# Weight conversion through a PSUM bank, its clamp on GpSimd, a small constant summed along a row, and early value products that take turns in one tile

## The chip, the cores and the metric

The kernel runs on one core of a Trainium2 chip. Five engines work there side by side, each through its own list of instructions in the order in which they stand: TensorE (PE in the profile, its weight loads PEld), VectorE (DVE), ScalarE (ACT), GpSimd (POOL) and SyncE (SP, which issues the DMAs). They wait for each other on semaphores. The metric is the device time of one execution in microseconds (us); less is better. Three runs of the kernel before gave 859.16, 859.77 and 861.7 us; the median, 859.77, is the time that the change is held against.

## What is computed

The reference is a local and global attention, whose result goes through a layer of three matrix products under a maximum, and one more product:

```python
s_g = scale * np.matmul(q_g, k_all.transpose(0, 1, 3, 2))        # 32 global queries, all 544 keys
out_g = np.matmul(sm(s_g), v_all)
s_ll = np.where(mask, scale * np.matmul(q_l, k_l^T), -1e9)       # 512 local queries, window of 32
a_l = sm(np.concatenate([s_lg, s_ll], axis=-1))                  # and the 32 global keys
out_l = np.matmul(a_l, np.concatenate([v_g, v_l], axis=2))
x = concat(out_g, out_l) as (8 * 544, 512)
h = np.maximum(np.maximum(x @ w1, x @ w2), x @ w3)               # 512 -> 768
out = h @ w_out                                                  # 768 -> 512
```

There are 8 batches of 8 heads of width 64. `sm` is the softmax, with 1e-9 added to the sum of each row before the division.

## The kernel before

**Places.** The attention is cut into 128 places (`sl` in the loop of line 533): two heads, 128 queries. A place takes the product of queries and keys (`scores`, L339 or L343), mask, minimum and exponent (L346 on DVE, L348 on ACT, which also sums the row into `z`), 1e-9 added to the sum (L350) and its reciprocal (L351), the scaling by it (`times`: L114 on DVE, L116 on ACT or L118 on POOL), a transposition on PE (`trans`, L367) that is copied out of PSUM into `pt`, and the product with the values (`pv`, L405 up to place 25, L412 after it), called PV below. The PV's result lies in the PSUM tile `O`, of two banks, and is copied to `xr` (L105 on ACT or L103 on DVE). `O` has one buffer: the next place's PV waits for that copy. Up to place 25 a PV writes only the first of the two banks. The global queries (`glob`, `glob_soft`, `transg`) go between.

**The layer.** `moe_group` runs the three products (L451), their maximum (L459) and the last product (L470). A matrix is held as a high part that PE's fp32r form takes and a rest (`wh` and `wl`, `woh` and `wol`), so that three matmuls make one product. Its matmuls are dealt out between those of the attention by `fill`; batch 0 goes in two halves of 256 columns, the first from place 8 on.

**The weights.** The 24 pieces (18 for `w1` to `w3`, 6 for `w_out`) come in the first 120 us as raw 64-bit words, two words of 32 bits for each of 512 numbers in 128 rows (`convert`, lines 146 to 168). ACT takes the absolute value of the high words into `wct` (L154). DVE clamps it between 2^-15 and the greatest allowed number (L157), masks and shifts it (L158), joins the sign (L159, written back over the high words of the raw tile `wraw`) and the bits of the low word (L160, into `wct`). ACT rounds the result to fp32r (L163), and POOL subtracts to get the rest (L166). Each call of `weight_step` moves each piece under way by one such step and starts the DMA of another. Three buffers of `wraw` and three of `wct` hold the pieces under way.

**What sets the order.** The code gives the order of the calls. A scheduler then orders each engine's instructions by its own times, with the calls as priorities, and sets the semaphores; it orders accesses of two engines to one tile after one another. Where an engine has a choice (`copy`, `sub`, `times`), the sums kept in `load` by `spend` and `least` choose it when the code is written out.

Of the kernel before, what the change touches and what calls it, by code (L numbers as in the profile page):

```python
# [10 lines left out]
F32 = mybir.dt.float32  # L11
F32R = mybir.dt.float32r
I32 = mybir.dt.int32
BF16 = mybir.dt.bfloat16
AF = mybir.ActivationFunctionType
ALU = mybir.AluOpType
AX = mybir.AxisListType
# [12 lines left out]
HIMAX = float(np.array(0x47EFFFFF, np.int32).view(np.float32))  # L30
# [20 lines left out]
def f32(ap):  # L51
    return ap.bitcast(F32)


def body(ctx, tc, kin, qin, vin, min_, win, out):
    nc = tc.nc
    act, dve, pool, pe = nc.scalar, nc.vector, nc.gpsimd, nc.tensor

    const = ctx.enter_context(tc.tile_pool(name="const", bufs=1))
    att = ctx.enter_context(tc.tile_pool(name="att", bufs=2))  # L60
    xp = ctx.enter_context(tc.tile_pool(name="xp", bufs=4))
    moe = ctx.enter_context(tc.tile_pool(name="moe", bufs=1))
# [3 lines left out]
    psO = ctx.enter_context(tc.tile_pool(name="psO", bufs=1, space=PSUM))  # L66

    small = ctx.enter_context(tc.tile_pool(name="small", bufs=4))
# [10 lines left out]
    def spend(e, ns):  # L79
        load[e] += ns  # L80
# [26 lines left out]
    def times(out, a, col, move=False):  # L107
        n = width(out)
        c = {"d": n * 0.52 + 125, "a": n * 0.833 + 185}
        if not move:  # L110
            c["p"] = n * 1.27 + 150
        e = least(c)
        if e == "d":
            dve.tensor_scalar(out=out, in0=a, scalar1=col, scalar2=None, op0=ALU.mult)  # L114
        elif e == "a":
            act.activation(out=out, in_=a, func=AF.Copy, scale=col)  # L116
        else:
            pool.tensor_scalar(out=out, in0=a, scalar1=col, scalar2=1.0, op0=ALU.mult, op1=ALU.mult)  # L118
# [5 lines left out]
    mask = const.tile([128, 2, 256], BF16, name="mask")  # L124
    zero = small.tile([128, 1], F32, name="zero", bufs=1)
    dve.memset(zero, 0.0)
    s4 = const.tile([128, 4, 2, 256], F32, name="s4")
    pool.memset(s4, 0.0)
    qgz = const.tile([128, 2, 160], F32R, name="qgz")
# [4 lines left out]
    wo = [const.tile([128, 6, DM], F32R, name=t) for t in ("woh", "wol")]  # L134
    xg = const.tile([128, NP, B, SG], F32, name="xg")


    def pieces():
        for n in range(24):
            f, i = divmod(n, 3)  # L140
            if n < 18:
                yield n, *[w[f][:, i].rearrange("p k f -> p (k f)") for w in (wh, wl)]
            else:
                yield n, *[w[:, n - 18] for w in wo]

    def convert(piece):
        m, dh, dl = piece
        r = moe.tile([128, 512], mybir.dt.int64, name="wraw", tag=f"h{3 + m % 3}")
        nc.sync.dma_start(out=r, in_=win[m])
        hi = r.bitcast(I32).rearrange("p (n t) -> p n t", t=2)[:, :, 1]  # L150
        lo = r.bitcast(I32).rearrange("p (n t) -> p n t", t=2)[:, :, 0]
        yield
        c = att.tile([128, 512], I32, name="wct", tag="vs") if m % 3 < 2 else moe.tile([128, 512], I32, name="wct")
        act.activation(out=f32(c), in_=r.bitcast(F32).rearrange("p (n t) -> p n t", t=2)[:, :, 1], func=AF.Abs)  # L154
        spend("a", 620)
        yield
        dve.tensor_scalar(out=f32(c), in0=f32(c), scalar1=2.0 ** -15, scalar2=HIMAX, op0=ALU.max, op1=ALU.min)  # L157
        dve.tensor_scalar(out=c, in0=c, scalar1=0x07FFFFFF, scalar2=3, op0=ALU.bitwise_and, op1=ALU.logical_shift_left)  # L158
        dve.scalar_tensor_tensor(out=hi, in0=hi, scalar=-0x40000000, in1=c, op0=ALU.bitwise_and, op1=ALU.bitwise_or)  # L159
        dve.scalar_tensor_tensor(out=c, in0=lo, scalar=29, in1=hi, op0=ALU.logical_shift_right, op1=ALU.bitwise_or)  # L160
        spend("d", 2300)
        yield
        act.copy(out=dh, in_=f32(c))  # L163
        spend("a", 615)
        yield
        pool.tensor_tensor(out=dl, in0=f32(c), in1=f32(dh), op=ALU.subtract)  # L166
        spend("p", 1350)
        yield True

    todo = pieces()  # L170
# [3 lines left out]
    def weight_load():  # L174
        piece = next(todo, None)
        if piece is not None:
            c = convert(piece)
            next(c)
            loaded.append(c)
# [11 lines left out]

    NAT = 26
    EARLY = 16
    kraw, kst, qraw, qs, vraw, vs, xr, sc, pg, pts, pgt = [{} for _ in range(11)]
    prob = []
    kn, qg = [], []
# [12 lines left out]
    def nat_k(p):  # L209
        if p < NP:  # L210
            return kn[p // 2][:, p % 2], qg[0][:, p]
        return kraw[p][:, 0:KW], kraw[p][:, KW:]
# [23 lines left out]
    def load_q(s):  # L236
        if s >= NS:
            return
        if s < EARLY:
            if s % 2 == 0:  # L240
# [76 lines left out]
    def scores(i):  # L317
        if i >= NS:
            return
        sl = ORDER[i]  # L320
        p, t = divmod(sl, 4)
        c0, n = WIN[t]

        ps = pm.tile([128, 512], F32, name="pm") if i < 8 else psS.tile([128, 512], F32, name="S")
        s = s4[:, i % 4]
        if i < EARLY:
            sc[i] = s
        else:
            if len(prob) < 2:
                prob.append(const.tile([128, 2, 256], F32R, name="prob", tag=f"prob{2 + len(prob)}"))  # L330
                pool.memset(f32(prob[-1]), 0.0)
            sc[i] = prob[i % 2]
        nm = small.tile([128, 2], F32, name="nm")
        z = small.tile([128, 2], F32, name="z")
        ph = [ps[:, 0:224], ps[:, 224:448]]
        for j in range(2):
            if i in NATK:

                pe.matmul(ph[j][:, 0:n], lhsT=qraw[i][:, 128 * j:128 * j + 128], rhs=nat_k(p)[0][:, c0:c0 + n],  # L339
                          start=True, stop=True)  # L340
                continue
            for a in range(2):
                pe.matmul(ph[j][:, 0:n], lhsT=qs[i][:, a, 128 * j:128 * j + 128],  # L343
                          rhs=kst[p][:, j, c0:c0 + n], start=(a == 0), stop=(a == 1))
        for j in range(2):
            dve.tensor_tensor_reduce(out=s[:, j, 0:n], in0=ph[j][:, 0:n], in1=mask[:, (1, 0, 1, 0)[t], 32 * (t == 0):32 * (t == 0) + n],  # L346
                                     scale=-0.125, scalar=3.0e38, op0=ALU.add, op1=ALU.min, accum_out=nm[:, j:j + 1])
            act.activation(out=s[:, j, 0:n], in_=s[:, j, 0:n], func=AF.Exp, bias=nm[:, j:j + 1], scale=-1.0,  # L348
                           accum_out=z[:, j:j + 1])
        dve.tensor_scalar(out=z, in0=z, scalar1=1e-9, scalar2=None, op0=ALU.add)  # L350
        dve.reciprocal(out=z, in_=z)  # L351
        for j in range(2):
            times(s[:, j, 0:n], s[:, j, 0:n], z[:, j:j + 1])
        if i >= EARLY:
            nc.sync.dma_start(out=f32(sc[i])[:, :, 0:n], in_=s[:, :, 0:n])
        spend("d", 2 * (n * 1.04 + 220) + 440)
        spend("a", 2 * (n * 0.833 + 278))

    def trans(sl):
# [3 lines left out]
        ps = psT.tile([128, 512], F32, name="T")  # L363
        pr, one = (ps, ident) if sl < EARLY else (ps.bitcast(F32R), identr)
        for j in range(2):
# [29 lines left out]
    def pv(sl):  # L395
        p, t = divmod(ORDER[sl], 4)
        pt = pts.pop(sl)
        o = psO.tile([128, 2, 512], F32, name="O")
        if t == 0:
            xr[p] = xp.tile([128, 4, 160], F32, name="xr")  # L400
        if sl < NAT:

            for c, j in ((0, 0), (0, 1), (1, 0), (1, 1)):
                n = 160 if c < GCH[t][2] else 128
                pe.matmul(o[64 * j:64 * j + 64, 0, 0:n], lhsT=vraw[sl][:, 2 * j + c], rhs=pt[:, j, c, 0:n], start=(c == 0), stop=(c == 1))  # L405
            copy(xr[p][:, t], o[:, 0, 0:160], True)
        else:

            for j in range(2):
                for c in range(2):  # L410
                    n = 160 if c < GCH[t][2] else 128
                    pe.matmul(o[:, j, 0:320].rearrange("p (a q) -> p a q", a=2)[:, :, 0:n],  # L412
                              lhsT=vs[sl][:, 2 * j + c].rearrange("p a d -> p (a d)"),
                              rhs=pt[:, j, c, :, 0:n], start=(c == 0), stop=(c == 1))
            lo = att.tile([64, 2, 160], F32, name="lox", bufs=1)
            copy(lo, o[64:128, :, 0:160], True)
            spend("d", 460 + 2 * 320)
            dve.tensor_tensor(out=lo, in0=o[0:64, :, 160:320], in1=lo, op=ALU.add)
            for j in range(2):
                dve.tensor_tensor(out=xr[p][64 * j:64 * j + 64, t], in0=o[0:64, j, 0:160], in1=lo[:, j], op=ALU.add)  # L420
        if t == 3:
            dve.tensor_reduce(out=xg[:, p % NP, p // NP], in_=xr[p][:, :, 128:160].rearrange("p t g -> p g t"),
                              axis=AX.X, op=ALU.add)
# [109 lines left out]
    for sl in range(NS):  # L533
        p, t = divmod(ORDER[sl], 4)
# [112 lines left out]
```

## Time and profile before

| what | before |
|---|---|
| median of three runs | 859.77 us |
| the profiled execution | 859.45 us |
| its span, first to last instruction | 857.4 us |
| PE busy | 814.9 us, 95% of the span |
| PE busy in the first 140 us | 106.4 us |
| DVE, ACT, POOL busy | 573.7, 530.8, 517.2 us |
| granted PE clock, mean | 0.981 |

How to read it: the profile is that of one execution. The span is what its instructions cover; 859.45 - 857.4 = 2.05 us lie around it. Busy shares are averages over a start (attention alone, with the weights being converted), a long middle part and an end (the layer alone). An engine's idle time matters only where the engine that sets the end waits for it. "Waited for" and releasers are inferred from the semaphores.

### The profile page before, as it was taken

What the parts mean: (1) busy time and instruction counts of PE and PEld (TensorE: products, weight loads), DVE (VectorE), ACT (ScalarE), POOL (GpSimd) and SP (SyncE); (2) the same over time, 40 slices, a digit from 0 to 9 for tenths busy, and PEclk for the clock granted to TensorE, in tenths of its full rate; (3) what the DMA queues carried; (4) which work ended last, traced back from release to release, by engine and by line L of the source; (5) the groups of instructions that cost most, each with busy time, mean ns of one, the idle gap of its engine ahead of it and who ended that gap; (6) DMA issues with size and microseconds to landing.
All of it is one profiled execution on the core that took longest, in us unless ns stands there. A gap on an engine that the chain in (4) does not pass through costs nothing.

```text
span 857.4 us, 15953 instructions
## 1 busy us (share of the span) xinstructions
PE 814.9 (95%) x4668; PEld 688.3 (80%) x4668; DVE 573.7 (67%) x1806; ACT 530.8 (62%) x1497; POOL 517.2 (60%) x705
## 2 busy tenths in 40 slices
PE   6668779989999999999999999999999999999997
PEld 4447668977888888888888888888888888888896
DVE  5889964587778677777777777867787776511111
ACT  6576555676677766767677767777776776511111
POOL 4578664687667666776678667766677664411211
PEclk9689899999999999999999999999999999999999
DMA  7555434444233533343333423253334332100000
GB/s 267 160 168 189 148 117 139 130 121 136 91 105 97 164 109 112 106 132 118 99 106 121 145 86 100 90 170 103 112 111 137 113 90 69 49 24 1 26 25 25
DMA packets 93414, 94.56 MB, mean 110 GB/s; under 512 B 18448, under 2 KB 81808, under 8 KB 93328
## 3 DMA queue, kind: packets, MB, share of 16 engines
q1 hardware_dynamic: 93328, 93.56, 35.3%
q8 instruction: 37, 0.61, 0.3%
q14 instruction: 49, 0.40, 0.2%
HBM read 56.85 MB, written 8.91 MB: 77 GB/s over the span
## 4 chain that ended last, share of the span: by engine, by line
PE 86%; DVE 7%; DMA 2%; issue 2%; ACT 1%; POOL 1%; SPq 0%; POOLq 0%; DVEq 0%; ACTq 0%
PE pm L451 48%; PE pm L470 16%; PE O L412 6%; PE S L343 5%; PE T L367 4%; PE S L287 2%; PE O L405 1%; DVE wct L160 1%; DVE wraw L159 1%; PE S L339 1%; DVE wct L157 1%; PE S L385 1%; PE S L283 1%; DVE z L350 1%; DVE s L346 1%
## 5 line engine op out<-in xcount | busy, mean ns | idle before, releaser
L451 PE MATMUL pm<-xs,wh 128*128 128x512 f32 (+1 forms) x1440 | 424.6, 370 | 8.8 <-DVE m L459 5.5
L451 PEld LDWEIGHTS pm<-xs,wh 128*128 128x128 f32 x1440 | 255.5, 191 | 40.4 <-DVE m L459 6.2
L451 PE MATMUL pm<-xs,wl 128*128 128x512 f32 (+1 forms) x720 | 266.6, 370 | 4.3 <-POOL wl L166 4.3
L118 POOL TENSOR_SCALAR s<-s,z 128x224 f32<-128x224 f32 (+1 forms) x248 | 114.7, 475 | 82.7 <-ACT lox L105 36.0
L451 PEld LDWEIGHTS pm<-xs,wl 128*128 128x128 f32 x720 | 137.4, 191 | 26.1 <-POOL wl L166 4.7
L470 PE MATMUL pm<-woh,h 128*128 128x512 f32 x408 | 133.7, 399 | 1.6 <-POOL h L97 1.2
L97 POOL TENSOR_TENSOR h<-m,h 128x512 fp32r<-128x512 f32 (+1 forms) x60 | 70.7, 1178 | 98.6 <-ACT h L105 98.5
L348 ACT ACTIVATE s<-s,nm 128x224 f32<-128x224 f32 (+1 forms) x256 | 118.2, 462 | 17.5 <-DVE nm L346 13.5
L459 DVE TENSOR_TENSOR m<-pm,m 128x512 f32<-128x512 f32 (+1 forms) x120 | 72.9, 608 | 71.2 <-PE pm L451 71.0
L97 POOL TENSOR_TENSOR qs<-qraw,qs 128x256 fp32r<-128x256 f32 x100 | 72.8, 738 | 54.7 <-ACT qs L105 45.5
L97 DVE TENSOR_TENSOR pt<-T,pt 128x512 fp32r<-128x512 f32 x102 | 70.4, 690 | 48.0 <-ACT pt L105 45.7
L346 DVE CUSTOM_DVE_ANT_0 s<-S,mask 128x224 f32<-128x224 f32 (+1 forms) x240 | 80.6, 370 | 23.3 <-PE S L339 17.7
L350 DVE TENSOR_SCALAR z<-z 128x2 f32<-128x2 f32 x128 | 55.8, 436 | 52.7 <-ACT s L348 52.5
L470 PEld LDWEIGHTS pm<-woh,h 128*128 128x128 f32 x408 | 74.6, 188 | 13.9 <-POOL h L97 1.7
L470 PE MATMUL pm<-wol,h 128*128 128x512 f32 x204 | 81.9, 401 | 0.0
L97 POOL TENSOR_TENSOR vs<-vraw,vs 128x256 fp32r<-128x256 f32 x102 | 75.5, 740 | 7.1 <-ACT vs L105 3.0
L97 POOL TENSOR_TENSOR kst<-kraw,kst 64x576 fp32r<-64x576 f32 x50 | 71.6, 1431 | 11.0 <-issue 7.0
L105 ACT CAST pt<-T 128x512 fp32r<-128x512 f32 x89 | 52.0, 584 | 39.3 <-PE T L367 39.3
L105 ACT CAST qs<-qraw 128x256 fp32r<-128x256 f32 x100 | 40.7, 407 | 56.1 <-PE S L343 51.8
L412 PEld LDWEIGHTS O<-pt,vs 128*128 128x128 f32 x408 | 66.1, 188 | 8.8
L412 PE MATMUL O<-pt,vs 128*128 128x320 f32 (+1 forms) x408 | 72.8, 300 | 0.0
L343 PEld LDWEIGHTS S<-kst,qs 128*128 128x128 f32 x400 | 59.3, 190 | 9.4 <-DVE nmg L291 1.1
(96 smaller groups left out, 1284.1 us busy)
## 6 DMA issues: line engine op xcount, KB each, us to landing
vraw<-v_in SPq DMA_DIRECT2D x64, 256.0 KB, 3.1
qraw<-q_in SPq DMA_DIRECT2D x100, 128.0 KB, 2.2
prob<-s SPq DMA_DIRECT2D x56, 224.0 KB, 2.4
wraw<-w_in SPq DMA_DIRECT2D x24, 512.0 KB, 3.6
prob<-s SPq DMA_DIRECT2D x56, 192.0 KB, 2.3
out_dram<-o SPq DMA_DIRECT2D x32, 256.0 KB, 2.4
kraw<-k_in SPq DMA_DIRECT2D x25, 320.0 KB, 3.0
qn<-q_in SPq DMA_DIRECT2D x8, 256.0 KB, 5.2
```

The lines of the kernel that those rows point to most:

```text
L97: (dve if least(c) == "d" else pool).tensor_tensor(out=out, in0=a, in1=b, op=ALU.subtract)
L105: act.copy(out=out, in_=a)
L118: pool.tensor_scalar(out=out, in0=a, scalar1=col, scalar2=1.0, op0=ALU.mult, op1=ALU.mult)
L343: pe.matmul(ph[j][:, 0:n], lhsT=qs[i][:, a, 128 * j:128 * j + 128], rhs=kst[p][:, j, c0:c0 + n], start=(a == 0), stop=(a == 1))
L346: dve.tensor_tensor_reduce(out=s[:, j, 0:n], in0=ph[j][:, 0:n], in1=mask[:, (1, 0, 1, 0)[t], 32 * (t == 0):32 * (t == 0) + n], scale=-0.12 ...
L348: act.activation(out=s[:, j, 0:n], in_=s[:, j, 0:n], func=AF.Exp, bias=nm[:, j:j + 1], scale=-1.0, accum_out=z[:, j:j + 1])
L350: dve.tensor_scalar(out=z, in0=z, scalar1=1e-9, scalar2=None, op0=ALU.add)
L367: pe.transpose(pr[:, 256 * j + 128 * c:256 * j + 128 * c + 128], s[:, j, 128 * c:128 * c + 128], one)
L412: pe.matmul(o[:, j, 0:320].rearrange("p (a q) -> p a q", a=2)[:, :, 0:n], lhsT=vs[sl][:, 2 * j + c].rearrange("p a d -> p (a d)"), rhs=pt[ ...
L451: pe.matmul(ps[:, 0:n], lhsT=w[f][:, i, k], rhs=xs[k][:, a, c0:c0 + n], start=(q == 0), stop=(q == 11))
L459: dve.tensor_tensor(out=m[:, 0:n], in0=ps[:, 0:n], in1=m[:, 0:n], op=ALU.max)
L470: pe.matmul(ps, lhsT=hh[f][:, a, 128 * t:128 * t + 128], rhs=w[:, f], start=(q == 0), stop=(q == 17))
```

## The change

Four edits. They are shown whole; the line numbers of the kernel after are larger by 4 to 12.

```diff
+    z8 = small.tile([128, 4, 2, 2], F32, name="z8", bufs=1)
+    dve.memset(z8, 1e-9)
...
+    early_o = psO.tile([128, 2, 512], F32, name="O")
...
-        c = att.tile([128, 512], I32, name="wct", tag="vs") if m % 3 < 2 else moe.tile([128, 512], I32, name="wct")
+        c = att.tile([128, 512], I32, name="wct", tag="vs") if m % 2 else moe.tile([128, 512], I32, name="wct", bufs=2)
...
-        dve.tensor_scalar(out=f32(c), in0=f32(c), scalar1=2.0 ** -15, scalar2=HIMAX, op0=ALU.max, op1=ALU.min)
-        dve.tensor_scalar(out=c, in0=c, scalar1=0x07FFFFFF, scalar2=3, op0=ALU.bitwise_and, op1=ALU.logical_shift_left)
-        dve.scalar_tensor_tensor(out=hi, in0=hi, scalar=-0x40000000, in1=c, op0=ALU.bitwise_and, op1=ALU.bitwise_or)
-        dve.scalar_tensor_tensor(out=c, in0=lo, scalar=29, in1=hi, op0=ALU.logical_shift_right, op1=ALU.bitwise_or)
-        spend("d", 2300)
+        pool.tensor_scalar(out=f32(c), in0=f32(c), scalar1=HIMAX, scalar2=2.0 ** -15, op0=ALU.min, op1=ALU.max)
+        spend("p", 800)
+        yield
+        w = early_o[:, 1].bitcast(I32)
+        dve.tensor_scalar(out=w, in0=c, scalar1=0x07FFFFFF, scalar2=3, op0=ALU.bitwise_and, op1=ALU.logical_shift_left)
+        dve.scalar_tensor_tensor(out=w, in0=hi, scalar=-0x40000000, in1=w, op0=ALU.bitwise_and, op1=ALU.bitwise_or)
+        dve.scalar_tensor_tensor(out=c, in0=lo, scalar=29, in1=w, op0=ALU.logical_shift_right, op1=ALU.bitwise_or)
+        spend("d", 2000)
         yield
...
-        spend("p", 1350)
+        spend("p", 1290)
...
+    EARLY_O = 18
...
+        ze = z8[:, i % 4]
...
-                           accum_out=z[:, j:j + 1])
-        dve.tensor_scalar(out=z, in0=z, scalar1=1e-9, scalar2=None, op0=ALU.add)
+                           accum_out=ze[:, j, 0:1])
+        dve.tensor_reduce(out=z, in_=ze, axis=AX.X, op=ALU.add)
...
-        o = psO.tile([128, 2, 512], F32, name="O")
+        if sl < EARLY_O:
+            o = early_o[:, :, 160 * (sl % 3):160 * (sl % 3) + 160]
+        else:
+            o = psO.tile([128, 2, 512], F32, name="O")
```

The clamp becomes a step of its own on POOL. The three bit operations stay on DVE, but their intermediate result `w` lies in the second bank of a tile `O` that is taken once, for places 0 to 17 together; the PVs of those places write its first bank, at one of three offsets by turns. There are four buffers of `wct` for three. The sum of a softmax row goes into the first of two numbers, the second of which is 1e-9, and a reduction adds the two. The global rows keep their addition (L301).

The scheduler's order is the same on PE from the PV of place 19 on, and changes ahead of that. On VectorE, before, the first conversion stands behind the exponents of the sixth pair of scores, and waits for ScalarE (its absolute value):

```order
L350 TENSOR_SCALAR z<-z 128x2 [waits Activation_49]
L299 TENSOR_TENSOR nmg<-nmg 64x1 [waits DVE_49]
L351 RECIPROCAL z<-z 128x2 [waits DVE_49]
L157 TENSOR_SCALAR wct<-wct 128x512 [waits Activation_49]
L158 TENSOR_SCALAR wct<-wct 128x512 [waits DVE_49]
L346 ISA s_92,nm<-pm,mask 128x192 [waits PE_49,Pool_49]
```

After (L165 to L167 are the three bit operations, L299 is L291 of before, L359 the new reduction; `O` stands for `w` in the second bank):

```order
L299 ISA sg,nmg<-S,zero 64x384 [waits PE_49,Pool_49]
L299 ISA nmg 64x1
L359 TENSOR_REDUCE z<-z_92 128x2 [waits Activation_49]
L299 ISA sg,nmg<-S,zero 64x160 [waits PE_49]
L165 TENSOR_SCALAR O<-wct 128x512 [waits Activation_49]
L360 RECIPROCAL z<-z 128x2 [waits DVE_49]
L166 SCALAR_TENSOR_TENSOR O<-wraw,O 128x512 [waits DMAHW1_49,DVE_49]
L167 SCALAR_TENSOR_TENSOR wct<-wraw,O 128x512 [waits DVE_49]
L165 TENSOR_SCALAR O<-wct 128x512 [waits DVE_49,Pool_49]
```

The first conversion has moved behind the second pair's global scores, and its wait for ScalarE is for the copy of place 2's PV out of the same tile `O`.

On TensorE, in the stretch in which the layer's matmuls have begun, a PV before (L405) waits for ScalarE, which fills `pt`:

```order
L451 MATMUL pm<-xs,wl_103 128x256
L451 MATMUL pm<-xs,wh_97 128x256
L405 MATMUL O<-pt,vraw 64x160 [waits PE_49,Activation_49]
L405 MATMUL O<-pt,vraw 64x160 x3
L451 MATMUL pm<-xs,wh_97 128x256
```

After, the PV (L417) of place 9 stands there, and the layer's matmuls are L463:

```order
L463 MATMUL pm<-xs,wh_100 128x256 x2
L463 MATMUL pm<-xs,wl_106 128x256
L417 MATMUL O<-pt,vraw 64x160 [waits DVE_49]
L417 MATMUL O<-pt,vraw 64x160 x3
L463 MATMUL pm<-xs,wh_100 128x256 x2
L463 MATMUL pm<-xs,wl_106 128x256 [waits Pool_49]
```

The PV now waits for VectorE: for the last bit operation (L167) of the conversion that stands ahead of it, which read the tile's other bank. That holds for the thirteen PVs of places 3 to 15, with 24 conversions between the PV of place 2 and that of place 15.

On VectorE the opposite wait stands after each of these PVs. Around place 8:

```order
L166 SCALAR_TENSOR_TENSOR O<-wraw,O 128x512 [waits DMAHW7_49,DVE_49]
L167 SCALAR_TENSOR_TENSOR wct<-wraw,O 128x512 [waits DVE_49]
L471 TENSOR_TENSOR m<-pm,m 128x256 [waits PE_49,Activation_49]
L471 TENSOR_TENSOR m<-pm,m 128x256 [waits DVE_49,PE_49]
L165 TENSOR_SCALAR O<-wct 128x512 [waits Activation_49,Pool_49]
L166 SCALAR_TENSOR_TENSOR O<-wraw,O 128x512 [waits DMAHW2_49,DVE_49]
```

L165 waits for ScalarE's copy of that PV into `xr`, and for POOL's clamp; between the two conversions stand two maxima of the layer (L471).

## The prediction

> **What bounds the kernel now.** I read the chain that ended last first, by engine, then the engines' busy time by stretch (span, PE, PEld, DVE, ACT, POOL, granted PE clock, DMA share, GB/s).
>
> ```profile
> span 857.4 us, 15953 instructions
> PE 86%; DVE 7%; DMA 2%; issue 2%; ACT 1%; POOL 1%; SPq 0%; POOLq 0%; DVEq 0%; ACTq 0%
> ```
>
> ```profile
> 17.00:122.60 105.60, 78.09 (x494) 61.71 (x492) 92.97 (x221) 67.51 (x185) 74.87 (x82) 0.85 0.49 156
> 27.20:122.60 95.40, 71.14 (x455) 57.34 (x453) 84.45 (x195) 60.88 (x165) 69.19 (x72) 0.86 0.49 156
> 0.00:140.00 140.00, 106.44 (x656) 83.39 (x658) 106.22 (x301) 85.77 (x243) 86.18 (x109) 0.89 0.54 172
> 140.00:200.00 60.00, 55.78 (x424) 49.79 (x421) 40.53 (x154) 41.44 (x130) 43.87 (x65) 1.00 0.42 125
> 200.00:740.00 540.00, 540.00 (x2989) 457.59 (x2988) 406.38 (x1311) 383.77 (x1085) 370.14 (x514) 1.00 0.37 112
> ```
>
> From 200 to 740 us PE is busy without a gap, so whatever the change does to the other engines there costs and gives nothing. PE is idle 33.6 us of the first 140, and in the stretch of the weight conversion (17 to 122.6) DVE is busy 92.97 of 105.6 us. That stretch sets the start; the 7% of DVE in the chain lie there. What DVE does in it by groups (count, busy us, mean ns); then DVE's busy time on the tile `wct` alone, which is the conversion, and last on everything in the first 10.2 us of the stretch:
>
> ```profile
> L160 DVE SCALAR_TENSOR_TENSOR wct<-wraw 128x512 int32<-128x512 int32 x24 | 23.7, 988 | 0.0
> L159 DVE SCALAR_TENSOR_TENSOR wraw<-wraw,wct 128x512 int32<-128x512 int32 x24 | 22.8, 948 | 0.3 <-DVE nm L346 0.2
> L157 DVE TENSOR_SCALAR wct<-wct 128x512 f32<-128x512 f32 x24 | 14.3, 595 | 2.0 <-ACT wct L154 2.0
> L158 DVE TENSOR_SCALAR wct<-wct 128x512 int32<-128x512 int32 x24 | 13.9, 580 | 0.2
> L346 DVE CUSTOM_DVE_ANT_0 s<-S,mask 128x224 f32<-128x224 f32 (+1 forms) x22 | 7.9, 363 | 3.3 <-PE S L339 3.3
> L350 DVE TENSOR_SCALAR z<-z 128x2 f32<-128x2 f32 x14 | 6.9, 491 | 2.2 <-ACT s L348 2.2
> ```
>
> ```profile
> 17.00:27.20 10.20, 5.58 (x7) 0.79 0.50 157
> 17.00:122.60 105.60, 72.44 (x96) 0.85 0.49 156
> ```
>
> ```profile
> 17.00:27.20 10.20, 8.52 (x26) 0.79 0.50 157
> ```
>
> 72.4 of 93 us are conversion. And it is slow for a reason that one place shows (start, duration):
>
> ```profile
> 29.95 0.69 DVE L159 SCALAR_TENSOR_TENSOR wraw<-wraw,wct 128x512 int32<-128x512 int32 x1
> ...
> 35.72 3.85 DVE L159 SCALAR_TENSOR_TENSOR wraw<-wraw,wct 128x512 int32<-128x512 int32 x1
> ```
>
> ```profile
> 35.38 1.17 POOL L118 TENSOR_SCALAR probg<-sg,zg 64x128 f32<-64x128 f32 x3
> 36.52 2.49 POOL L166 TENSOR_TENSOR wl<-wct,wh 128x512 fp32r<-128x512 f32 x2
> ```
>
> The same operation takes 0.69 or 3.85 us; the long one ends at 39.57, one plain duration after POOL's work ended at 39.01. DVE waited for POOL inside the instruction.
>
> **The change part by part.** I follow PE to the PV of place 19, from which PE's order is the same: in before it starts at 139.58. What comes earlier there, comes earlier at the end.
>
> ```profile
> 139.58 0.76 PE L405 MATMUL O<-pt,vraw 128*64 128x160 f32 x8
> ```
>
> Prices of nearest rows (count, busy us, mean ns; the last with min/median/max):
>
> ```profile
> L459 DVE TENSOR_TENSOR m<-pm,m 128x512 f32<-128x512 f32 x84 | 57.9, 689 | 50.0 <-PE pm L451 49.9
> L350 DVE TENSOR_SCALAR z<-z 128x2 f32<-128x2 f32 x128 | 55.8, 436 | 52.7 <-ACT s L348 52.5
> ...
> L346 DVE DVE_READ_ACCUMULATOR2_ANT nm<- 128x1 f32 x256 | 21.0, 82 | 0.0
> L351 DVE RECIPROCAL z<-z 128x2 f32<-128x2 f32 x128 | 21.0, 164 | 3.6
> ...
> L422 DVE TENSOR_REDUCE xg<-xr 128x32 f32<-128x128 f32 x32 | 12.3, 384 | 0.5
> ...
> L103 DVE COPY pt<-T 128x512 f32<-128x512 f32 x1 | 0.7, 692 | 0.6 <-PE T L367 0.6
> ```
>
> ```profile
> L118 POOL TENSOR_SCALAR sg<-sg,zg 64x544 f32<-64x544 f32 x28 | 20.0, 714 | 28.2 <-ACT pt L105 26.0 <-DVE zg L302 1.1 <-ACT sg L300 0.7
> ```
>
> ```profile
> L157 DVE TENSOR_SCALAR wct<-wct x24: 395/416/1860, 17.9 to 114.9; 128x512 f32<-128x512 f32 x24
> L163 ACT CAST wh<-wct x18: 602/619/622, 22.4 to 97.0; 128x512 fp32r<-128x512 f32 x18
> L166 POOL TENSOR_TENSOR wl<-wct,wh x18: 1254/1442/1816, 24.2 to 97.7; 128x512 fp32r<-128x512 f32 x18
> ```
>
> Bit operations. Each now has at most one input in SBUF, as L459 has, whose mean is its plain duration. I take 0.69 for all three (the first between 0.42, the median of such an operation inside SBUF, and 0.69): 24 x 2.07 = 49.7 us for 72.4. The Trainium skill (VectorE: DVE Perf Modes, "Why PSUM operands drop a tier") says that an operand in PSUM costs a 4-byte operation its double rate; by that the low end falls away, and at the low end the sum would be 6.6 us shorter.
>
> Sum of the rows. No row shows a reduction of 2 x 2 numbers; between nothing and 0.38 I take the reciprocal's 0.16, since fixed cost is all that it has: 14 x (0.491 - 0.16) = 4.6 us off DVE. Of the 128 in all, the 114 later ones lie beside a full PE; without that cover they would be worth 30 us ((55.8 - 6.9) - 114 x 0.16).
>
> Other work of DVE from 27.2 on is (92.97 - 72.44) - (8.52 - 5.58) = 17.6 us, less 4.6. By the order four more masked scores stand ahead of the last conversion: 4 x (0.363 + 0.08, the short read that follows each) = 1.8. So DVE has 49.7 + 14.8 = 64.5 us to do. Its idle time of that stretch, 95.40 - 84.45 = 10.95, I keep.
>
> The later start. The first conversion now waits for the copy of place 2's PV, which ended at 27.46 in before:
>
> ```profile
> 27.17 0.29 ACT L105 COPY xr<-O 128x160 f32<-128x160 f32 x1 [3.57 <-PE O L405]
> ```
>
> So I start at 27.5, where before 5.58 us of conversion were done; this is in the sum, since all 24 stand behind it.
>
> The new wait. Conversion and PV exclude each other in the shared tile. A PV waits for L167, with PE's layer matmuls and the next scores queued behind it; the next L165 waits for the copy of that PV, with the maxima and later scores queued on DVE, for which ACT's exponents wait. One such turn in before, PV to copy:
>
> ```profile
> 67.99 0.76 PE L405 MATMUL O<-pt,vraw 128*64 128x160 f32 x8
> ...
> 69.14 0.28 ACT L105 COPY xr<-O 128x160 f32<-128x160 f32 x1
> ```
>
> 1.43 us; with the hand-overs 1.5, thirteen times 19.5. By the order 2 to 8 other instructions of DVE stand between the last conversion ahead of a PV and the next one behind it, and go on meanwhile, so I take half, 9.75 (bounds 0 and 19.5). The offsets by turns save nothing: a PV still waits, now for more.
>
> The clamp on POOL. 24 x 0.71 = 17.0 us (544 columns in 64 rows take 714 ns; no row has a minimum on POOL; at the subtraction's 1.25 it would be 30). POOL had 31 us idle between 17 and 122.6. Behind a clamp queue subtractions and scalings; DVE waits for it. I take a quarter, 4.3, as standing in DVE's way (bounds 0 and 17.0). ACT's added scalings and the memset hide in ACT's and DVE's idle time; a fourth `wct` buffer costs nothing. SP's load of the next `wraw` waits for L167 as it did for L160, with the loads of queries and values behind it: no change.
>
> Sum: 27.5 + 64.5 + 10.95 + 9.75 + 4.3 = 117.0 us for the last subtraction, where before it ended at 122.1:
>
> ```profile
> 120.85 1.28 POOL L166 TENSOR_TENSOR wol<-wct,woh 128x512 fp32r<-128x512 f32 x1
> ```
>
> But PE is then further: by the order 49 matmuls stand between the first that waits for that subtraction and the PV of place 19. In before the PV of place 17 began at 129.69, with 59 matmuls to go, 9.89 us; 49 take 8.2.
>
> ```profile
> 129.69 0.76 PE L405 MATMUL O<-pt,vraw 128*64 128x160 f32 x8
> ```
>
> PE's own 71.1 us at clock 0.86 fit. The PV comes at 125.2 for 139.58, 14.4 us earlier, and PE is full from 200 on: 859.45 - 14.4 = 845.05 for the profiled execution; the median of the runs is 0.32 above it: **845.4 us**.
>
> **The rivals.** Turns uncovered (chance 0.18): all 19.5 us, 9.75 more: 855.2. For it: each engine's order is fixed, so an engine that finds one instruction blocked can't take the next first. Against: the instructions between.
>
> Turns covered (0.15): half of the 14.05 us for turns and clamps goes: 838.4; all of it, 831.4.
>
> The ring, slower (0.11): a piece's clamp stands on POOL behind an earlier piece's subtraction, that behind ACT's rounding, that behind DVE's bit operations, and DVE's next piece waits for the clamp: 0.62 + 1.25 + 0.71 = 2.6 us each turn with nothing between, 33.8 in all in place of the 4.3: 874.9. It decides from 1.6 us of such waiting in each turn on ((14.4 + 2.6 + 4.3)/13). Against: by the order clamps stand a piece or more ahead of their use.
>
> The port pays back (0.06): the 17.0 us given to POOL block DVE for as long, as in the 3.85 us above, instead of 4.3: 858.1, no change. The rows speak against it: few DVE operations of that stretch keep two inputs in SBUF. The Trainium skill (Perfetto Trace Analysis, "Optimizing Scalar/DVE Operations") warns that work moved between GPSIMD and DVE may not help, since they share a read port. The 3.85 us agree with the shared port, not with the conclusion.
>
> **How the numbers follow.** The forecast has 0.50. 0.3%, 2.6 us, is about what a measurement can tell from no change. Faster: 0.50 + 0.18 + 0.15 = 0.83; same 0.06; slower 0.11. The range 836 to 857 leaves out the ring, the port and the far part of covered turns, together 0.2.
>
> **What would show it.** Right: L166 and L167 at 0.69 us with no long ones, the reduction below 0.2, the clamp at 0.7, DVE's conversions near 50 us, the PV of place 19 near 125 and PE full from 200 on. The new wait must show as PE's wait for L167 (DVE) before PVs and DVE's wait for ACT's copy or for POOL before L165. Wrong: bit operations that still stretch to microseconds (the port), DVE waiting for the clamp over 1.6 us a turn (the ring), or a gain in the first 140 us that is lost after it.

## The result and the profile after

The kernel after takes 849.1 us (median of four runs, 849.05 to 850.82), the kernel before on the same chip 859.46 (four runs, 858.21 to 861.7). The ratio is 0.9881, with a 95% interval from 0.9857 to 0.9906: 10.4 us faster. The forecast was 845.4 us, with a range from 836 to 857. The profiled execution of after is its longest run, 850.82 us, 8.6 less than that of before.

The page of after gives its span, and the share by engine of the chain that ended last:

```profile
span 848.8 us, 15999 instructions
PE 81%; DVE 2%; DMA 1%; ACT 1%; POOL 1%; issue 1%; SPq 0%; POOLq 0%; ACTq 0%; DVEq 0%
```

The windows of after (columns as in the prediction: PE, PEld, DVE, ACT, POOL, PE clock, DMA share, GB/s):

```profile
17.00:122.60 105.60, 86.05 (x540) 66.69 (x536) 71.24 (x221) 71.49 (x201) 72.57 (x105) 0.90 0.52 164
27.20:122.60 95.40, 78.27 (x493) 61.29 (x493) 66.15 (x191) 64.11 (x177) 66.41 (x92) 0.91 0.54 170
0.00:140.00 140.00, 115.01 (x724) 88.54 (x726) 85.54 (x297) 90.67 (x260) 88.11 (x137) 0.93 0.56 179
200.00:740.00 540.00, 540.00 (x2985) 457.62 (x2984) 380.50 (x1302) 379.98 (x1077) 365.64 (x509) 1.00 0.36 110
```

DVE lost 21.7 us of work in the conversion stretch (92.97 to 71.24), PE is idle 25.0 us of the first 140 for 33.6, and the long middle is as full as before. The DVE groups of that stretch show why (count, busy us, mean ns; then idle time ahead of them):

```profile
L166 DVE SCALAR_TENSOR_TENSOR O<-wraw,O 128x512 int32<-128x512 int32 x24 | 16.6, 692 | 0.3
L165 DVE TENSOR_SCALAR O<-wct 128x512 int32<-128x512 int32 x24 | 16.6, 690 | 5.9 <-POOL s L118 2.1 <-issue 1.9 <-ACT xr L105 0.9
L167 DVE SCALAR_TENSOR_TENSOR wct<-wraw,O 128x512 int32<-128x512 int32 x24 | 16.4, 683 | 0.4
...
L359 DVE TENSOR_REDUCE z<-z 128x2 f32<-128x4 f32 x17 | 2.6, 151 | 0.2
```

All three bit operations take 0.69 us, each time; nothing is stretched to microseconds. And yet the last subtraction ends no earlier, at 122.64 us for 122.13, and the PV of place 19 comes at 131.02. Its timeline rows on POOL and on PE:

```profile
121.36 1.28 POOL L173 TENSOR_TENSOR wol<-wct,woh 128x512 fp32r<-128x512 f32 x1
```

```profile
131.02 0.76 PE L417 MATMUL O<-pt,vraw 128*64 128x160 f32 x8
```

That PV is 8.56 us earlier than before, and the execution 8.63 us shorter. So the whole gain lies ahead of place 19, as forecast, but it is 8.6 and not 14.4. DVE is now idle for 34 of the 105.6 us, so something besides its work holds up the start.

### The profile page after: what moved, and what is told of

The parts are those of the page before. It is cut to its first block, busy times and chain, and to the rows that moved or that the text cites. A ratio compares the mean times of both kernels' runs of the same rounds, so it can differ in the third digit from the quotient of the medians.

```text
span 848.8 us, 15999 instructions
## 1 busy us (share of the span) xinstructions
PE 814.9 (96%) x4668; PEld 685.8 (81%) x4668; DVE 523.8 (62%) x1784; ACT 530.4 (62%) x1498; POOL 515.4 (61%) x727
## 4 chain that ended last, share of the span: by engine, by line
PE 81%; DVE 2%; DMA 1%; ACT 1%; POOL 1%; issue 1%; SPq 0%; POOLq 0%; ACTq 0%; DVEq 0%
PE pm L463 47%; PE pm L482 15%; PE O L424 6%; PE S L352 5%; PE T L376 4%; PE S L295 2%; DMA prob<-s 1%; PE S L394 1%; PE O L417 1%; PE S L348 1%; ACT s L357 0%; DVE xr L432 0%; DVE pt L97 0%; ACT sg L308 0%; DVE s L355 0%
## 5 line engine op out<-in xcount | busy, mean ns | idle before, releaser
L463 PE MATMUL pm<-xs,wh 128*128 128x512 f32 (+1 forms) x1440 | 419.9, 367 | 2.7 <-ACT wh L170 2.4
L463 PEld LDWEIGHTS pm<-xs,wh 128*128 128x128 f32 x1440 | 252.6, 189 | 33.3 <-ACT wh L170 2.9
L463 PE MATMUL pm<-xs,wl 128*128 128x512 f32 (+1 forms) x720 | 266.0, 370 | 3.9 <-POOL wl L173 3.8
L463 PEld LDWEIGHTS pm<-xs,wl 128*128 128x128 f32 x720 | 136.1, 189 | 25.7 <-POOL wl L173 5.2
L118 POOL TENSOR_SCALAR s<-s,z 128x224 f32<-128x224 f32 (+1 forms) x246 | 105.6, 442 | 63.8 <-ACT lox L105 40.6
L97 POOL TENSOR_TENSOR h<-m,h 128x512 fp32r<-128x512 f32 (+1 forms) x60 | 68.7, 1145 | 99.0 <-ACT h L105 98.7
L471 DVE TENSOR_TENSOR m<-pm,m 128x512 f32<-128x512 f32 (+1 forms) x120 | 73.0, 608 | 77.6 <-PE pm L463 75.5
L432 DVE TENSOR_TENSOR xr<-O,lox 64x160 f32<-64x160 f32 x204 | 64.3, 315 | 3.4
```

What stands on the lines that cost most here:

```text
L97: (dve if least(c) == "d" else pool).tensor_tensor(out=out, in0=a, in1=b, op=ALU.subtract)
L463: pe.matmul(ps[:, 0:n], lhsT=w[f][:, i, k], rhs=xs[k][:, a, c0:c0 + n], start=(q == 0), stop=(q == 11))
L471: dve.tensor_tensor(out=m[:, 0:n], in0=ps[:, 0:n], in1=m[:, 0:n], op=ALU.max)
```

## The experiments

Four theories of what holds it up. A: PE with its own work sets the pace. B: the turns that conversions and PVs take in the shared tile `O`, which nothing covers. C: the clamp delays POOL's subtractions. D: it is still DVE's list of work, as the forecast summed it. Medians with the kernel before on the same chip, and the ratio's 95% interval:

| run | edit | us | before | ratio |
|---|---|---|---|---|
| after | the change | 849.1 | 859.5 | 0.986 to 0.991 |
| e1 | after, bit operations in a bank of their own | 837.1 | 859.6 | 0.972 to 0.975 |
| e2 | after, no clamp | 853.2 | 859.6 | 0.991 to 0.995 |
| e3 | after, two bit operations of three | 838.6 | 859.6 | 0.974 to 0.978 |
| e4 | after, clamp on DVE | 858.9 | 859.6 | 0.998 to 1.001 |
| e5 | e1, two bit operations of three | 838.6 | 860.1 | 0.973 to 0.977 |
| e6 | before, clamp on POOL alone | 862.8 | 860.1 | 1.002 to 1.005 |
| e7 | before, new sum of 1e-9 alone | 856.9 | 860.1 | 0.996 to 0.998 |
| e8 | before, bit operations through a bank of their own alone | 847.7 | 860.1 | 0.983 to 0.988 |
| e9 | e1, clamp on DVE | 846.1 | 859.5 | 0.982 to 0.986 |
| e10 | e1, old sum of 1e-9 | 837.4 | 859.5 | 0.972 to 0.976 |
| e11 | before, the turns alone | 860.3 | 859.5 | 0.999 to 1.002 |

**e1: no turns.**

```diff
...
-    early_o = psO.tile([128, 2, 512], F32, name="O")
+    early_o = psE.tile([128, 512], F32, name="Oe")
+    early_w = psE.tile([128, 512], F32, name="We")
...
-        w = early_o[:, 1].bitcast(I32)
+        w = early_w.bitcast(I32)
...
```

`psE` is a pool of two banks that is closed ahead of place 18, where `psO` opens in its stead.

> The change as it is, but the early value products and the bit operations get a PSUM tile of one bank each, so that neither waits for the other; nothing else is edited. The change as it is: 849.1 us, the value product of place 19 at 131.0 us. Theory A (pace): after the change TensorE with its own work sets the pace from place 7 on (53.8 of 60.5 us busy between the products of places 7 and 15), and the 5.7 us that the forecast lacks lie there; the turns cost only what the trace shows, 1.4 us of TensorE's wait for the last bit operation: 847.5 to 849.5 us, place 19 not before 129. Theory B (turns): the 5.7 us are turns that nothing covers: 843 to 844.5 us, place 19 near 125.

It took 837.1 us, 12 less than the change. Theory A falls at once, as far as the change goes, and the gain is more than twice the 5.7 us that theory B had counted. The windows of e1, up to the end of its last subtraction and over the first 140 us; then that subtraction on POOL and the PV of place 19 on PE:

```profile
27.20:104.90 77.70, 67.64 (x478) 55.46 (x477) 61.37 (x183) 61.81 (x176) 64.61 (x91) 0.96 0.65 201
...
0.00:140.00 140.00, 122.03 (x839) 99.43 (x840) 90.20 (x330) 97.94 (x287) 95.00 (x150) 0.96 0.62 195
```

```profile
103.63 1.28 POOL L176 TENSOR_TENSOR wol<-wct,woh 128x512 fp32r<-128x512 f32 x1 [1.27 <-ACT woh L173]
```

```profile
116.81 0.76 PE L424 MATMUL O<-pt,vraw 128*64 128x160 f32 x8
```

The last subtraction ends at 104.91, 17.7 us earlier than in the change, and place 19 comes 14.2 us earlier, as much as the span is shorter (834.4 for 848.8). DVE's idle time from 27.2 to that subtraction falls from 29.25 (95.40 - 66.15) to 16.33 us (77.70 - 61.37); the other 4.8 us are work of DVE that no longer stands in that stretch. In part that is because e1 starts its first conversion at 19.1 and not at 27.0 us: 2.7 us of conversions lie ahead of 27.2 there, 0.2 in the change. So e1 gives back all that the shared tile costs, the later start with it, and not the turns alone. How the turns cost that much shows in one of them, in the timeline of the change around the PV of place 12 (all engines; the rows between are left out):

```profile
96.06 0.68 DVE L167 SCALAR_TENSOR_TENSOR wct<-wraw,O 128x512 int32<-128x512 int32 x1
...
97.45 0.28 PE L463 MATMUL pm<-xs,wl 128*128 128x256 f32 x1
...
97.66 0.71 PE L417 MATMUL O<-pt,vraw 128*64 128x160 f32 x8
...
98.24 0.67 ACT L158 ACTIVATE wct<-wraw 128x512 f32<-128x512 f32 x1 [0.47 <-DMA wraw<-w_in]
...
98.81 0.28 ACT L105 COPY xr<-O 128x160 f32<-128x160 f32 x1
...
99.18 0.69 DVE L165 TENSOR_SCALAR O<-wct 128x512 int32<-128x512 int32 x1 [0.92 <-ACT xr L105]
```

The conversion lets go of the tile at 96.74, and the next begins at 99.18. In the 2.44 us between, PE first ends the layer's matmuls that stand ahead of the PV, and ACT's copy stands behind an absolute value that waits for its DMA. Little of this is booked as a wait for the turn: PE works, ACT waits for a DMA, and DVE's row shows 0.92 us. So the waits that the profile puts down to the turns are far less than what they cost: 0.9 us of DVE for the copy (the row of L165 above), and of PE and its weight loads for L167 what the view of that line names (who waited, us, times):

```profile
  PEld O L417: 1.8, 2
  PE O L417: 1.4, 2
```

The tile's own account shows it. From the first matmul of place 2's PV to the end of place 15's copy are 97.6 us:

```profile
24.25 0.53 PE L417 MATMUL O<-pt,vraw 128*64 128x160 f32 x1
```

```profile
121.62 0.27 ACT L105 COPY xr<-O 128x160 f32<-128x160 f32 x1
```

Summing from each L165's start to its L167's end, and from each PV's start to its copy's end, the 24 conversions hold the tile for 56.4 us (2.35 each) and the 14 PVs for 21.2 (1.51 each): 77.6 of 97.6 us. That is a larger share than DVE's 66, POOL's 66 or ACT's 64 of 95.4; only PE's 78 is larger, and e1, where place 19 comes 14.2 us earlier, shows that PE could go faster. The rest are hand-overs like this one. In e1 PV and conversion lie side by side:

```profile
73.57 0.71 PE L424 MATMUL Oe<-pt,vraw 128*64 128x160 f32 x8
...
73.72 0.69 DVE L170 SCALAR_TENSOR_TENSOR wct<-wraw,We 128x512 int32<-128x512 int32 x1
...
74.52 0.69 DVE L168 TENSOR_SCALAR We<-wct 128x512 int32<-128x512 int32 x1
...
75.98 0.31 ACT L107 COPY xr<-Oe 128x160 f32<-128x160 f32 x1
```

Here the copy comes 2.41 us after its PV's start, later than in the change, and costs nothing, since DVE goes on. In the change too the two lie in different banks of the tile; it is the scheduler that orders them by the tile. The Trainium skill (PSUM — Partial Sum Buffer, "PSUM bank collisions raise a hardware error") asks for semaphores by bank and quadrant, in the simple version by bank. e1, in which PE and DVE work in two banks at the same time, agrees. The wait gone, the earlier start and the order that the scheduler then writes come together in e1. How much each gives wasn't taken apart.

**e3 and e5: one bit operation less, with and without turns.** Both leave out the second operation, which joins the sign, and book 1310 for 2000 in `spend`.

```diff
...
-        dve.scalar_tensor_tensor(out=w, in0=hi, scalar=-0x40000000, in1=w, op0=ALU.bitwise_and, op1=ALU.bitwise_or)
...
-        spend("d", 2000)
+        spend("d", 1310)
...
```

> The change as it is with one of the three bit operations left out (the second, which joins the sign): VectorE loses 24 x 0.69 = 16.6 us in the conversion. Theory A (pace): VectorE is no longer what bounds the start, so little comes of it: 847 to 849.2. Theory D (the forecast's own sum, VectorE's list as the line that sets the end): 16.6 us less on that line, of which TensorE's idle 6.7 us between places 7 and 15 and what it idles before allow at least 6: 843 or less.

> The kernel of e1 (the change with a PSUM tile of its own for the bit operations, 837.1 us) with the second bit operation left out, as in e3: VectorE loses the same 16.6 us that gave 10.5 us with the shared tile. New theory B (the shared tile is the line that sets the end: it is held 77.7 of the 97.6 us from the value product of place 2 to that of place 15, and e3 gained because each hold became 0.7 us shorter): without the shared tile VectorE's price counts for little: 834 to 837. Theory D (VectorE's list sets the end, with or without turns): about 10 us again: 825 to 829.

With the shared tile it gives 10.5 us (838.6), without it nothing (838.6 for 837.1), about as theory B expected. But this doesn't settle what e3 gained by. The windows of e5 up to the end of its last subtraction and from there to the PV of place 19, those two rows, and the window of e1 between its own two:

```profile
27.20:98.02 70.82, 60.96 (x444) 50.57 (x442) 54.66 (x172) 56.08 (x154) 58.65 (x79) 0.96 0.62 205
98.00:117.80 19.80, 18.07 (x118) 14.57 (x116) 7.07 (x36) 7.72 (x25) 3.16 (x7) 1.00 0.45 135
```

```profile
96.72 1.29 POOL L175 TENSOR_TENSOR wol<-wct,woh 128x512 fp32r<-128x512 f32 x1 [0.49 <-ACT woh L172]
```

```profile
117.80 0.76 PE L423 MATMUL O<-pt,vraw 128*64 128x160 f32 x8
```

```profile
104.90:116.80 11.90, 11.83 (x82) 10.17 (x82) 3.37 (x22) 6.56 (x20) 2.45 (x6) 1.00 0.45 135
```

The last subtraction of e5 ends at 98.01, 6.9 us earlier than in e1; only place 19 comes no earlier (117.80 for 116.81). In between PE is busy 18.07 of 19.80 us, in e1 11.83 of 11.90: there PE's own work sets the end, and an earlier conversion no longer shows in it. Nor did DVE lose 16.6 us. With less booked in `spend`, the code deals it more copies, scalings and subtractions, and up to the last subtraction it is busy 54.66 us for e1's 61.37, 6.7 less. DVE also waits longer for POOL's clamp, as the first bit operation's group shows in e1 and in e5:

```profile
L168 DVE TENSOR_SCALAR We<-wct 128x512 int32<-128x512 int32 x24 | 16.6, 690 | 10.2 <-POOL wct L164 10.1
```

```profile
L168 DVE TENSOR_SCALAR We<-wct 128x512 int32<-128x512 int32 x24 | 16.5, 689 | 13.9 <-POOL wct L164 13.8
```

So e3's 10.5 us can come from shorter holds of the tile (theory B) or from less work in DVE's list (theory D): each operation that stands in a hold stands in that list too. That sharing the tile costs the change about 12 us rests on e1 alone, and needs neither.

**e2: no clamp.**

```diff
-        pool.tensor_scalar(out=f32(c), in0=f32(c), scalar1=HIMAX, scalar2=2.0 ** -15, op0=ALU.min, op1=ALU.max)
-        spend("p", 800)
```

> The change as it is without the clamp (left out: numbers below 2^-15 or above the greatest allowed are not clamped), the step in which it stood kept empty. GpSimd loses 24 x 0.615 = 14.8 us. Theory A (pace): TensorE's waits for GpSimd's subtraction (3.8 and 2.5 us in the first 140) shrink in part, 1 to 3 us: 846 to 848. Theory C (GpSimd): the clamp delays every subtraction and with it the pieces; all of the 6.3 us of waits go: 842 to 844.

It took 853.2, 4.1 us more than the change (2.5 between the two profiled executions): neither A nor C expected that. Theory C falls, for with 14.8 us less to do POOL gave nothing back. What made it longer isn't settled. Part of it is one hold of the tile: ahead of the PV of place 15 DVE waits inside a conversion, for a matmul, in the change and in e2 (timelines of DVE):

```profile
119.40 0.32 DVE L299 CUSTOM_DVE_ANT_0 sg<-S,zero 64x160 f32<-64x160 f32 x1 [0.35 <-PE S L291]
```

```profile
121.95 0.32 DVE L297 CUSTOM_DVE_ANT_0 sg<-S,zero 64x160 f32<-64x160 f32 x1 [1.44 <-PE S L289]
```

That is 1.1 us. A hold lasts as long as DVE's list between its first and last operation, with whatever that waits for.

**e4 and e9: the clamp back on DVE, with and without turns.**

```diff
-        pool.tensor_scalar(out=f32(c), in0=f32(c), scalar1=HIMAX, scalar2=2.0 ** -15, op0=ALU.min, op1=ALU.max)
-        spend("p", 800)
+        dve.tensor_scalar(out=f32(c), in0=f32(c), scalar1=2.0 ** -15, scalar2=HIMAX, op0=ALU.max, op1=ALU.min)
+        spend("d", 420)
```

> The change as it is, with the clamp back on VectorE inside SBUF as in the kernel before, in the step of its own that GpSimd had. VectorE gains 24 x 0.42 to 0.60 = 10 to 14 us, GpSimd loses 14.8. Theory A (pace): VectorE has 34 us idle in the conversion stretch, and takes it at little cost: 847.5 to 851. Theory C (GpSimd): the relief counts: 843 to 846. Theory D (VectorE's line): 10 to 14 us longer: 858 or more.

> The kernel of e1 (own bank for the bit operations, 837.1 us) with the clamp back on VectorE, in its own step. If, with the turns gone, VectorE's price counts for little (as e5 says of 16.6 us less), 16.4 us more (24 x 0.68, as in e8) stay mostly hidden: 837 to 841 us. Rival: e8 (847.7), which differs from e1 by the clamp and the sum of 1e-9, says that VectorE is close to being the bound again, so that the clamp makes most of these 10.6 us: 844 to 848.

e4 is 9.8 us longer than the change, e9 9.0 longer than e1. e4's 858.9 is what theory D expected, and e9's 846.1 what its rival did. The clamp doesn't touch the tile, so with the shared tile, too, DVE's list counts; part of its cost comes through the tile, whose conversions hold it for 60.9 us in e4 and 56.4 in the change. So D doesn't fall: the tile's holds and DVE's list lengthen each other. e1 stands about where the bound passes from the conversion to PE's own work: an earlier conversion gave nothing in e5, and 16.9 us more of DVE's work cost 9 in e9. The group of the clamp in e9 (count, busy us, mean ns, idle time ahead):

```profile
L164 DVE TENSOR_SCALAR wct<-wct 128x512 f32<-128x512 f32 x24 | 16.9, 705 | 5.8 <-ACT wct L161 5.6
```

**e6: the clamp on POOL alone.** The kernel before with the clamp's lines of the change, the fourth buffer, and the bit operations in SBUF.

> The kernel before (859.6 us) with the clamp alone on GpSimd, in a step of its own and with the fourth buffer; the bit operations stay inside SBUF. Rival of the prediction (the port pays back): the 14.8 us more of GpSimd's work block VectorE's operations with two inputs in SBUF for as long, as the 14.3 us of the clamp leave VectorE: 857 to 862. The forecast's sum (VectorE's line, less 14.3, plus 4.3): 849 to 851.

862.8 us, 2.7 more than before. Its DVE groups:

```profile
L161 DVE SCALAR_TENSOR_TENSOR wraw<-wraw,wct 128x512 int32<-128x512 int32 x24 | 30.4, 1265 | 0.5
L162 DVE SCALAR_TENSOR_TENSOR wct<-wraw 128x512 int32<-128x512 int32 x23 | 17.9, 780 | 0.2
L160 DVE TENSOR_SCALAR wct<-wct 128x512 int32<-128x512 int32 x24 | 16.1, 670 | 12.8 <-POOL wct L157 12.8
```

Of the two operations with both inputs in SBUF, one went from 948 to 1265 ns and the other from 988 to 780, and the first bit operation from 580 to 670: together some 5 us more. DVE's wait for the clamp, 12.8 us, is the larger part: waiting, and to a lesser degree stretching, take back the 14.3 us that the clamp had cost DVE. The Trainium skill (Perfetto Trace Analysis, "Optimizing Scalar/DVE Operations") says that work moved between GPSIMD and DVE may not help. e6 agrees in its time, though most of what it lost is waiting for the clamp; with the bit operations in PSUM the same move is worth 9.8 us (e4 against the change), and there the measurement decides.

**e7 and e10: the sum of 1e-9.** e7 is the kernel before with the lines of `z8`, `ze` and the reduction alone; e10 is e1 without them.

> The kernel before (859.6 us) with the new sum of 1e-9 alone. The forecast's term: 14 operations of 0.491 become 0.15 in the conversion stretch, 4.8 us less on VectorE's line, which sets the end there: 854 to 856; the other 114 lie beside a full TensorE and give nothing. Rival: most of these 0.491 us are a wait for GpSimd, which the next operation with two inputs in SBUF then has instead: 858 to 860.

> The kernel of e1 (837.1 us) with the sum of 1e-9 as it was in the kernel before. Hidden under TensorE as VectorE's other work is in e1: 836.5 to 839. Rival: it counts as it did alone in e7 (3.2 us) or more, and the rest of e8's distance: 840 to 845.

3.2 us in the kernel before, nothing (0.3) in e1. In e7 the sum takes 2.2 us for 15, where before 14 took 6.9, but the bit operations' first one rises from 580 to 740 ns, and DVE's time on the tile `wct` from 72.44 to 78.90 us. So the conversion got longer by more than the sum had saved; where the 3.2 us come from is not shown.

```profile
L160 DVE TENSOR_SCALAR wct<-wct 128x512 int32<-128x512 int32 x24 | 17.8, 740 | 0.2
...
L353 DVE TENSOR_REDUCE z<-z 128x2 f32<-128x4 f32 x15 | 2.2, 145 | 0.2 <-ACT s L351 0.2
```

**e8: PSUM alone.** e1's tiles with the clamp on DVE, in the step and with the buffers of the kernel before, and the old sum.

> The kernel before (859.6 us) with the bit operations through PSUM alone, in a bank of their own, so that there are no turns; the clamp stays on VectorE, the sum of 1e-9 as before. Theory B (turns are what the change lost): bit operations 58.1 + 14.3 become 49.7 + 14.3 us at least, and the kernel gains 8 to 14 us: 845 to 852. Rival: without the clamp on GpSimd most of the gain is gone, since the clamp and the small sums now take the stretched durations that the bit operations had: 855 to 860.

847.7 us; its runs lie further apart than the others' (843.5 to 852). Its rival falls: the bit operations through PSUM are worth 12.4 us by themselves, about as much as the whole change brought (the intervals overlap).

**e11: turns alone.** The kernel before with `early_o` and its three offsets for the PVs; nothing else writes the tile.

```diff
...
+        if sl < EARLY_O:
+            o = early_o[:, :, 160 * (sl % 3):160 * (sl % 3) + 160]
...
```

> The kernel before (859.6 us) with the early value products in one tile by turns alone; the bit operations stay in SBUF, so that nothing else writes the tile. Theory B: the tile costs only where conversions write it too, and the value products took turns in one buffer before as well: 858.5 to 861.5. Rival: placing them at three offsets in one tile changes the time by itself, by over 3 us either way.

860.3 for 859.5: no difference. The tile costs only where the conversions write it too.

## Why the prediction was right, and where its size was off

| step | forecast | measured |
|---|---|---|
| first conversion starts | 27.5 | 27.0 |
| bit operations, 24 pieces | 49.7 us | 49.6 (16.6 + 16.6 + 16.4) |
| DVE's work from there on | 64.5 us | 66.15 |
| DVE's idle time: kept, turns, clamp | 10.95 + 9.75 + 4.3 = 25.0 us | 29.25 |
| last subtraction ends | 117.0 | 122.64 |
| from there to the PV of place 19 | 8.2 us | 8.4 |
| gain at that PV | 14.4 us | 8.56 |
| gain of the profiled execution | the same | 8.63 |

Right were the bound (DVE's conversion, stretched by POOL), its cure (no bit operation has two inputs in SBUF, and none is stretched), the prices 0.69 and 0.16 us (measured 0.69 and 0.151), the start, the last stretch on PE, and that what place 19 gains the end gains. The clamp took 0.616 us and not 0.71. The rule of the Trainium skill (VectorE: DVE Perf Modes, "Why PSUM operands drop a tier") and the trace agree: L165 has no row below 0.680 us, where L157 inside SBUF went down to 0.395. One reading was loose: the operation of 3.85 us ends 0.56 us after POOL's work, which is less than its plain 0.69, so that the pair doesn't time the wait exactly.

The step that was off is the one on the turns: "so I take half, 9.75 (bounds 0 and 19.5)". The last subtraction comes 5.6 us later than forecast, and by the table 4.25 of them are idle time of DVE and 1.65 its work. e1 splits the idle time: 16.33 us are left without turns, near the 10.95 + 4.3 = 15.25 that the forecast kept for the rest, and 12.92 go with them, two thirds of 19.5 and not half. All that the shared tile costs, with the later start that the forecast had priced by itself, is 17.7 us at the last subtraction, and 14.2 at the PV of place 19, ahead of which PE is full in e1. The reason given for half, that 2 to 8 other instructions of DVE go on meanwhile, bears less than that: in the turn shown above DVE works for some 0.5 of the 2.44 us between two conversions, and waits for the rest. The forecast's line, DVE's list, still adds up in the change; the tile, held for 77.6 of 97.6 us, is what puts the idle time into it. That is the rival "turns uncovered" in its mechanism. Its price, 855.2, was too high, since of its 19.5 us only those 12.92 show: DVE's idle time came to 29.25 and not to 34.75. The clamp's 4.3 by itself isn't to be had back: e2, without it, was no faster. That the two kept terms come out near 16.33 is in part luck, for in e1 10.1 us of waits are for the clamp alone.

The ring isn't seen in the change: the row of L165 names no wait for a clamp. In e1 it is (10.1 us of DVE's waits for L164), without deciding, as e5's 13.8 us at about the same time show. The port that pays back showed in e6 alone, with the bit operations in SBUF, and there DVE's wait for the clamp (12.8 us) weighs more than the stretching (5). The waits named under "what would show it" came as foreseen, PE for L167 and DVE for ACT's copy, and would have misled: 1.4 and 0.9 us stand for a cost of 12 to 14.

## What to carry to other kernels

When two engines' work is put into one buffer, add up how long each user holds it, from first write to last read with all that waits in between, as one adds up an engine's busy time; the buffer can hold up every engine while none is busy all the time, and its waits are then booked to whatever stands in each queue. Before sharing, see whether the users can have a bank each: here that (e1, 837.1 us, ratio 0.9737, interval 0.9722 to 0.9751) beat both kernels. And try each part both alone and with the others: the clamp on POOL cost 2.7 us alone and was worth 9 to 10 beside the bit operations in PSUM; the new sum was worth 3.2 us alone and nothing in e1.

## What the runs showed of the hardware

POOL's operations, too, are shorter where the bit operations go through PSUM. Its groups in the change, for the conversion stretch (columns as above):

```profile
L161 POOL TENSOR_SCALAR wct<-wct 128x512 f32<-128x512 f32 x24 | 14.8, 616 | 8.4 <-ACT wct L158 7.4
L118 POOL TENSOR_SCALAR s<-s,z 128x192 f32<-128x192 f32 (+1 forms) x29 | 12.5, 443 | 8.1 <-DVE z L360 2.4 <-issue 2.2 <-DVE nmg L307 1.6
```

In e6, with the bit operations in SBUF, the same clamp takes 753 ns and the same scaling 698:

```profile
L157 POOL TENSOR_SCALAR wct<-wct 128x512 f32<-128x512 f32 x24 | 18.0, 753 | 5.2 <-ACT wct L154 3.8
L118 POOL TENSOR_SCALAR s<-s,z 128x192 f32<-128x192 f32 (+1 forms) x25 | 17.2, 698 | 8.7 <-DVE z L353 7.2 <-ACT xr L105 1.0
```

A reduction of four numbers in each row to two takes DVE 0.151 us. PE's granted clock over the first 140 us is 0.89 in before (106.4 us busy), 0.93 in the change (115.0) and 0.96 in e1 (122.0). It doesn't follow that busy time alone: e3 has 121.6 us at 0.93. What lowers it wasn't tried.
